# Block means of V as products with a constant matrix, in a three-stage attention and feed-forward kernel

## The chip, the cores and the metric

The kernel runs on one core of a Trainium2 chip. The metric is the device time of one execution in microseconds. TensorE (PE in the profile) does the matrix products, VectorE (DVE), ScalarE (ACT) and GpSimd (POOL) the element-wise work, and SyncE (SP) issues nearly all loads and stores.

## The reference, cut to what matters

```python
B, H, S, D = 2, 8, 768, 64;  block, window = 32, 16
k_sum = k.reshape(B, H, 24, 32, D).max(axis=3)      # block maxima
v_sum = v.reshape(B, H, 24, 32, D).mean(axis=3)     # block means
scores_l = q @ k.T / 8      # kept where |i - j| < 16, else -1e9
scores_s = q @ k_sum.T / 8 + log(32)
a = softmax(concat(scores_l, scores_s))
x = a @ concat(v, v_sum)                            # 1536 x 512 over both batches
h = x @ w_in;  x = (h - tanh(h)) @ w_out            # 512 -> 2048 -> 512
xn = rms_norm(x) * rms_g
out = (silu(xn @ w_gate) * (xn @ w_val)) @ w_out2   # 512 -> 1536 -> 512
```

The change touches only the block means of V in the first batch, the order of the block maxima of K in the second, and the order of the first loads.

## The kernel before, in words

**Attention.** The 1536 rows are twelve tiles of 128 queries, six for each batch. A *unit* is one tile and one parity of the heads (four heads): unit 2i is tile i with parity 0, unit 2i+1 the same tile with parity 1. `scores(u)` multiplies the tile's queries (a load `q` of 512 KB for each tile) with a window of 96 keys and the 24 block maxima (`kw`), four heads of 120 columns each, in true 32-bit (L347; each product is two instructions on PE). VectorE adds the mask and takes the row's extreme (L350), ScalarE takes the exponential (L352), VectorE finishes the sums (L353, L354), GpSimd scales (L355). `trans(u)` turns the result on PE (L362), ScalarE copies it out (L367), and `pv(i)` multiplies both parities with the tile's window of V (`v`, L379). `pv` writes x as a rounded half (ScalarE, L382) and a remainder (VectorE, L383).

**Block maxima of K.** `ksum_a(b, par, hf)` loads half the tiles of one parity (`kw`, 576 KB) and takes the maxima on VectorE (L264, two L266, L267). `ksum_b` spreads them over the partitions by two products with a selection matrix (L273), and VectorE and GpSimd write them into `kw`. No unit of a parity can start before both halves of its maxima.

**Block means of V.** `vsum_a(b, c)` loads a quarter of V (`vt`, 384 KB, features on the partitions) and adds up 32 neighbours. For the first batch quarters 0, 2 and 3 are one VectorE reduction each (L295), and quarter 1 is a tree of additions on GpSimd (L291, L293). `vsum_b` turns the four quarters on PE (L301), and ScalarE (L305) and VectorE (L307) scale by 1/32 and write the 24 rows into the tile's `v`. `pv(0)` needs both.

**Feed-forward.** Weights come as 64-bit words and are decoded into two rounded parts: ScalarE L163, VectorE L164, L165 and L166, the rounding on VectorE (L173, the first four pieces) or ScalarE (L171), the remainder on GpSimd (L174). Loads of weights go through three buffers `raw`. `up_step` (L396 to L398) is a product of 384 columns for a group of three tiles, so the first needs `pv` of tiles 0, 1 and 2 and the first decoded weight; `down_step` (L402 to L404) has 512 columns. Both are in the rounded format, one instruction for each product.

**Order.** Each task has a due time in `plan`; tasks are emitted in the order of their due times, each behind the tasks that it requires. A scheduler with a timeline model then fixes each engine's order at build time, and each engine runs its list in order. Loads that wait for nothing go out in the order of emission. The first four units are due in the order 0, 2, 1, 3 (`ORD`), at 6, 9.5, 13 and 15.5; unit 4 is due at 18.

Of the kernel before, what the change touches and what calls it, by code (L numbers as in the profile page):

```python
# [2 lines left out]

# [50 lines left out]
TP1 = 1.0  # L54
TC = 0.6
TK01 = 1
TV = 4
TK1 = -8
TV1 = -8
TD0 = 11  # L60
# [6 lines left out]
PSV = 0  # L67
PTV = 0
KBUF = 4
PVS = (1, 1)  # L70
PB = 4
PTB = 3
SHIFT = {}
ALT = ()
OSA = 6
SSH = 8
TSEL = 0.3
TQ = (0.2, 3)
TVL = (6, 16)
ORD = [0, 2, 1, 3]  # L80
TKB = (4, 6)
VE = ((0, 1, 0, 0), (1, 1, 1, 1))
DTV = 0.25
TVS = 10
TCKW = {"schedule_with_timeline_sim": True}


# [1 line left out]
def attn_moe_kernel(ctx: ExitStack, tc: tile.TileContext, ins, out, dbg=None):  # L89
    nc = tc.nc  # L90
    V, A, G, T = nc.vector, nc.scalar, nc.gpsimd, nc.tensor

    cst = ctx.enter_context(tc.tile_pool(name="cst", bufs=1))
    wp = ctx.enter_context(tc.tile_pool(name="wp", bufs=SLOTS_A))
# [9 lines left out]
    ps_t = att_ctx.enter_context(tc.tile_pool(name="ps_t", bufs=PST, space=PSUM))  # L104
    ap1 = att_ctx.enter_context(tc.tile_pool(name="ap1", bufs=1))
# [3 lines left out]
    kp_ = att_ctx.enter_context(tc.tile_pool(name="kp", bufs=KBUF))  # L109
    sa = att_ctx.enter_context(tc.tile_pool(name="sa", bufs=4))  # L110
    rawp = att_ctx.enter_context(tc.tile_pool(name="rawp", bufs=RB))
    state = {}

    def f(ap):
        return ap.bitcast(F32)

    sel = cst.tile([128, 256], F32, name="sel")
    ident = sel[:, 64:192]
    rg = cst.tile([128, KD], F32, name="rg")
    mask = ap1.tile([128, 3, WID], F32, name="mask")  # L120


    def consts():
        nc.sync.dma_start(out=mask, in_=ins["mask"])
        nc.sync.dma_start(out=rg, in_=ins["rms_g"])


    jobs = []
# [120 lines left out]
    def ksum_a(b, par, hf):  # L249
        if not kwin:  # L250
            for h2 in range(2):
                for p2 in range(2):
                    kwin[0, p2, h2] = kp_.tile([128, KT, 4 * WID], F32, name="kw")
        if b:
            kwin[b, par, hf] = kp_.tile([128, KT, 4 * WID], F32, name="kw")
        kw = kwin[b, par, hf]
        m1 = ap2.tile([128, KT, 2, 4], F32, name="m1")
        m2 = ap2.tile([128, KT, 2, 4], F32, name="m2")
        if not hf:
            kmax[b, par] = ap2.tile([128, 4, TPB, 2], F32, name="mx")  # L260
        ts = slice(hf * KT, hf * KT + KT)
        nc.sync.dma_start(out=kw[:, :, 0:4 * LOC], in_=ins["kw"][b, par, :, ts])
        w = kw[:, :, 0:4 * LOC].rearrange("p t (j k c) -> p t j k c", j=4, k=4)
        V.tensor_reduce(m1.rearrange("p t j k -> p t (j k)"), kw[:, :, 96:288].rearrange("p t (x c) -> p t x c", c=24), AX.X, ALU.max)  # L264
        for j in range(2):
            V.tensor_reduce(m2[:, :, j], w[:, :, 3 * j, :, 16:24], AX.X, ALU.max)  # L266
        V.tensor_tensor(kmax[b, par][:, :, ts].rearrange("p k t j -> p t j k"), m1, m2, ALU.max)  # L267

    def ksum_b(b, par):
        mx = kmax.pop((b, par)).rearrange("p k t j -> p (k t j)")  # L270
# [5 lines left out]
        G.tensor_copy(sm[:, 1:], sm[:, 0:1].to_broadcast([128, KT - 1, 96]))  # L276
        G.tensor_copy(sm2, sm[:, 0:1].to_broadcast([128, KT, 96]))

    def vsum_a(b, c, pool, name):
# [3 lines left out]
        raw = pool.tile([128, 1024], U32, name=name) if name == "raw" else pool.tile([128, 2, 512], F32R, name=name).rearrange("p a n -> p (a n)")  # L283
        rr = f(raw)[:, 0:S]
        nc.sync.dma_start(out=rr, in_=ins["vt"][b, c])
        r = rr.rearrange("p (n j) -> p n j", j=BLK)
        o = vt_[b][:, c, LOC:]
        if VE[b][c]:
            n = BLK // 2
            while n > 1:  # L290
                G.tensor_tensor(r[:, :, 0:n], r[:, :, 0:n], r[:, :, n:2 * n], ALU.add)  # L291
                n //= 2
            G.tensor_tensor(o, r[:, :, 0], r[:, :, 1], ALU.add)  # L293
        else:
            V.tensor_reduce(o, r, AX.X, ALU.add)  # L295

    def vsum_b(b):
        vt = vt_.pop(b)
        ps = ps_t.tile([128, 512], F32, name="t")
        for c in range(4):  # L300
            T.transpose(ps[0:WID, c * 128:(c + 1) * 128], vt[:, c], ident)  # L301
        if b == 0:
            v_of[0] = 0
            vsum[b] = v_b[0][LOC:WID, 0]
            A.activation(v_b[0][LOC:WID, 0], ps[LOC:WID], AF.Copy, scale=1.0 / BLK)  # L305
            if PVS[b]:
                V.tensor_scalar(v_b[0][LOC:WID, 1], ps[LOC:WID], 1.0 / BLK, None, ALU.mult)  # L307
            else:
                A.activation(v_b[0][LOC:WID, 1], ps[LOC:WID], AF.Copy, scale=1.0 / BLK)
            return  # L310
        vsum[b] = ap1.tile([128, DM], F32, name="vsum")[LOC:WID]
        if PVS[b]:
            V.tensor_scalar(vsum[b], ps[LOC:WID], 1.0 / BLK, None, ALU.mult)
        else:
            A.activation(vsum[b], ps[LOC:WID], AF.Copy, scale=1.0 / BLK)
# [18 lines left out]
    def scores(u):  # L334
        b, t, par = unit(u)
        q = q_b[(u // 2) % QB]
        kw = kwin[b, par, t // KT][:, t % KT].rearrange("p (j k c) -> p j k c", j=5, k=4)
        mk = mask[:, 1 if 0 < t < TPB - 1 else (0 if t == 0 else 2)]
        P = Pp.tile([128, 4, WID], F32, name="P")
        nb = sp.tile([128, 4], F32, name="nb")  # L340
        sm = sp.tile([128, 4], F32, name="sm")
        nh = 2 if (u < S2) != (f"sh{u}" in ALT) else 4
        for k0 in range(0, 4, nh):
            ps = ps_h.tile([128, 512], F32, name="h") if u < SSH else ps_t.tile([128, 512], F32, name="t")
            for i in range(nh):
                k = k0 + i
                T.matmul(ps[:, i * WID:(i + 1) * WID], q[:, 4 * par + k], kw[:, :, k], start=True, stop=True)  # L347
            for i in range(nh):
                k = k0 + i
                V.tensor_tensor_reduce(P[:, k], ps[:, i * WID:(i + 1) * WID], mk, -0.125, 3e38, ALU.add, ALU.min, nb[:, k:k + 1])  # L350
# [37 lines left out]
    for j, nch in enumerate(NCH):  # L388
# [4 lines left out]
    acc, part, gs, last = {}, {}, {}, {}  # L393
# [200 lines left out]
    def task(key, at, fn, *req):  # L594
        plan[key] = (at + SHIFT.get(key, 0), len(plan), fn, req)
# [48 lines left out]
    at = TM0  # L644
# [61 lines left out]
    for i in range(n0, len(steps) + LAG):  # L706
# [18 lines left out]
        j, g, m, first, end = steps[i - LAG]  # L725
# [5 lines left out]
        if j == len(NCH) - 1 and end:  # L731
            t = free["t"]
# [33 lines left out]
        down2(*prev, j)  # L766


_INS = ["q", "kw", "vt", "vw", "mask", "sel", "rms_g", "w_in", "w_out", "w_gate", "w_val", "w_out2"]


def layouts(q, k, v, moe_w_in, moe_w_out, moe2_w_gate, moe2_w_val, moe2_w_out, moe2_rms_g):
# [15 lines left out]
    vt = v.transpose(0, 2, 1, 3).reshape(B, S, DM)  # L788
# [45 lines left out]
```

## Time and profile before

| what | us |
|---|---|
| median of three runs | 655.16 (654.47 to 655.91) |
| the profiled execution | 655.48 |
| its span, first to last instruction | 653.7 |
| PE busy | 625.3 (96% of the span) |
| VectorE busy | 455.1 (70%) |
| ScalarE busy | 325.6 (50%) |
| GpSimd busy | 232.4 (36%) |

Busy time is an average over stages with different limits: which engine or transfer ends the waits has to be read for each stretch by itself. A busy PE may also be one that runs at half its clock.

### The profile page before, as it was taken

How to read it: one execution, taken by the hardware profiler on the slowest of the kernel's cores; microseconds unless marked ns; L12 is line 12 of the kernel's file. 1: busy time of each engine (PE TensorE's matmuls, PEld its weight loads, DVE VectorE, ACT ScalarE, POOL GpSimd, SP SyncE). 2: the span in 40 equal slices, each digit the busy share in tenths (PEclk: the TensorE clock that was granted, in tenths of full speed). 3: DMA queues.
4: the chain of work that ended last, by engine and by line, in shares of the span. 5: the costliest groups of instructions: out<-in, count | busy, mean ns of one | idle time of the engine just before them, and what ended most of it. 6: DMA issues, size and time to landing. Idle time of an engine off the chain costs nothing.

```text
span 653.7 us, 9841 instructions
## 1 busy us (share of the span) xinstructions
PE 625.3 (96%) x3576; PEld 570.3 (87%) x3576; DVE 455.1 (70%) x979; ACT 325.6 (50%) x783; POOL 232.4 (36%) x237
## 2 busy tenths in 40 slices
PE   3878999999999999999999899999999999999997
PEld 3768898889999999999998887999999999999995
DVE  5899755458777667766458488676778768778644
ACT  2865576545543444444456765454544544454420
POOL 1467721113231223441000026545626645555300
PEclk9878999999999999999999899999999999999999
DMA  9986321123222223111000001021111211111013
GB/s 331 348 259 238 110 99 50 46 77 130 99 107 85 100 94 129 66 65 64 1 2 0 2 33 65 33 98 64 66 65 64 97 66 64 66 66 64 2 65 128
DMA packets 19641, 58.92 MB, mean 90 GB/s; under 512 B 2168, under 2 KB 5496, under 8 KB 19592
## 3 DMA queue, kind: packets, MB, share of 16 engines
q1 hardware_dynamic: 19592, 58.29, 25.9%
q8 instruction: 28, 0.46, 0.3%
q14 instruction: 21, 0.17, 0.1%
HBM read 54.84 MB, written 3.15 MB: 89 GB/s over the span
## 4 chain that ended last, share of the span: by engine, by line
PE 74%; issue 12%; DVE 9%; ACT 2%; DMA 1%; POOL 1%; SPq 0%; DVEq 0%; POOLq 0%
PE h L398 7%; PE h L396 7%; PE h L397 7%; PE acc L403 5%; PE acc L402 5%; PE acc L404 5%; PE t L402 5%; PE t L403 5%; PE t L404 5%; PE acc L396 4%; PE acc L397 4%; PE acc L398 4%; PE accx L397 2%; PE accx L396 2%; PE accx L398 2%
## 5 line engine op out<-in xcount | busy, mean ns | idle before, releaser
L174 POOL TENSOR_TENSOR w<-dt,w 128x512 fp32r<-128x512 f32 (+1 forms) x59 | 75.8, 1284 | 147.0 <-ACT w L171 120.6
L398 PE MATMUL h<-x,w 128*128 128x384 f32 x248 | 84.3, 341 | 2.2 <-DVE x L383 2.2
L396 PE MATMUL h<-x,w 128*128 128x384 f32 x248 | 85.0, 343 | 0.9 <-ACT x L382 0.9
L397 PE MATMUL h<-x,w 128*128 128x384 f32 x248 | 84.3, 340 | 0.0
L414 ACT ACTIVATE s<-h 128x384 f32<-128x384 f32 x64 | 31.2, 487 | 75.9 <-PE h L398 75.6
L415 DVE TENSOR_TENSOR s<-h,s 128x384 f32<-128x384 f32 x64 | 35.5, 554 | 40.8 <-ACT s L414 40.2
L396 PE MATMUL acc<-x,w 128*128 128x384 f32 x168 | 57.6, 343 | 2.7 <-ACT s L530 1.9
L165 DVE SCALAR_TENSOR_TENSOR dt<-da,dt 128x512 uint32<-128x512 uint32 x68 | 55.9, 823 | 5.2 <-ACT da L163 1.4
L418 DVE TENSOR_TENSOR g<-s,g 128x384 fp32r<-128x384 f32 x64 | 44.5, 696 | 21.5 <-ACT g L417 21.4
L438 DVE TENSOR_TENSOR part<-t,part 128x512 f32<-128x512 f32 x60 | 40.5, 686 | 26.3 <-PE t L404 26.1
L397 PE MATMUL acc<-x,w 128*128 128x384 f32 x168 | 57.3, 341 | 0.0
L166 DVE SCALAR_TENSOR_TENSOR dt<-raw,dt 128x512 uint32<-128x512 uint32 x68 | 56.1, 826 | 1.3
L403 PE MATMUL acc<-w,g 128*128 128x512 f32 x144 | 57.0, 396 | 0.0
L403 PE MATMUL t<-w,g 128*128 128x512 f32 x144 | 56.8, 395 | 0.0
L404 PE MATMUL t<-w,g 128*128 128x512 f32 x144 | 56.7, 393 | 0.0
L404 PE MATMUL acc<-w,g 128*128 128x512 f32 x144 | 56.4, 396 | 0.0
L398 PE MATMUL acc<-x,w 128*128 128x384 f32 x168 | 56.3, 340 | 0.0
L402 PE MATMUL t<-w,g 128*128 128x512 f32 x144 | 55.2, 397 | 1.1 <-DVE part L436 0.8
L402 PE MATMUL acc<-w,g 128*128 128x512 f32 x144 | 54.5, 395 | 0.0
L526 DVE TENSOR_TENSOR g<-s,g 128x384 fp32r<-128x384 f32 x48 | 33.4, 708 | 25.9 <-ACT g L525 25.9
L352 ACT ACTIVATE P<-P,nb 128x120 f32<-128x120 f32 x96 | 36.8, 384 | 28.2 <-DVE nb L350 27.7
L396 PEld LDWEIGHTS h<-x,w 128*128 128x128 f32 x248 | 47.1, 190 | 3.6 <-ACT x L382 1.3
(130 smaller groups left out, 1556.7 us busy)
## 6 DMA issues: line engine op xcount, KB each, us to landing
raw<-w_out SPq DMA_DIRECT2D x28, 512.0 KB, 3.2
raw<-w_in SPq DMA_DIRECT2D x16, 512.0 KB, 3.8
q<-q SPq DMA_DIRECT2D x12, 512.0 KB, 7.6
raw<-w_gate SPq DMA_DIRECT2D x12, 512.0 KB, 3.1
raw<-w_val SPq DMA_DIRECT2D x12, 512.0 KB, 3.4
kw<-kw SPq DMA_DIRECT2D x8, 576.0 KB, 6.7
v<-vw SPq DMA_DIRECT2D x12, 384.0 KB, 5.1
out_dram<-part SPq DMA_DIRECT2D x12, 256.0 KB, 2.0
```

Of the source, the lines that this page charges most:

```text
L165: V.scalar_tensor_tensor(t, a.bitcast(U32), 3, t, ALU.logical_shift_left, ALU.bitwise_or)
L166: V.scalar_tensor_tensor(t, r[:, :, 1], 0x80000000, t, ALU.bitwise_and, ALU.bitwise_or)
L174: G.tensor_tensor(lo, d, f(hi), ALU.subtract)
L352: A.activation(P[:, k], P[:, k], AF.Exp, scale=-1.0, bias=nb[:, k:k + 1], accum_out=sm[:, k:k + 1])
L396: T.matmul(o, wh, xh, start=start, stop=False, **kw)
L397: T.matmul(o, wl, xh, start=False, stop=False, **kw)
L398: last["PE"] = T.matmul(o, wh, xl, start=False, stop=stop, **kw)
L402: T.matmul(o, g[:, 0, js], w[:, 0], start=first, stop=False)
L403: T.matmul(o, g[:, 1, js], w[:, 0], start=False, stop=False)
L404: last["PE"] = T.matmul(o, g[:, 0, js], w[:, 1], start=False, stop=end)
L418: last["DVE"] = V.tensor_tensor(gg[:, 1], t, f(gg[:, 0]), ALU.subtract)
L438: V.tensor_tensor(part[t], a, part[t], ALU.add)
```

## The change

The block means of the first batch are no longer reduced on VectorE and GpSimd. V is loaded in its natural layout, keys on the partitions, in three pieces `vn` of 512 KB, and each of the six tiles of 128 keys is multiplied by a slice of a constant matrix `mean` (128 x 130, holding 1/32 at the right places). The six products of 512 columns, in true 32-bit, add up in one accumulator; ScalarE and VectorE copy it out as before, without the scaling. `tc.issue_after(ins)` puts the instructions of its block behind `ins` in the order of that instruction's engine; it adds no semaphore. The six products are put behind the last score product emitted so far, which with the due time 15.6 is that of the fourth unit; the maxima of the second batch are put behind the last L350 emitted so far.

The loads change order. Before: `kw` (parity 0, first half), `q` of tile 0, `kw` (second half), `sel`, `mask`, `rg`, two `kw` of parity 1, `q` of tile 1, four `vt`, `vw` of tile 0, `q` of tile 2, weights. After: `kw` first half on SyncE and second half on ScalarE's queue, `sel`, `q` of tile 0, `mask`, two `kw` of parity 1, `mean`, three `vn`, `vw` of tile 0, `q` of tile 1, `q` of tile 2, weights; `rg` at 20.

```diff
-TV = 4
+TV = 1.5
-TSEL = 0.3
-TQ = (0.2, 3)
-TVL = (6, 16)
+TSEL = 0.15
+TQ = (0.4, 3)
+TVL = (2.6, 16)
-TVS = 10
+TVS = 15.6
...
 def ksum_a(b, par, hf):
-        nc.sync.dma_start(out=kw[:, :, 0:4 * LOC], in_=ins["kw"][b, par, :, ts])
+        (nc.scalar if not (b or par) and hf else nc.sync).dma_start(out=kw[:, :, 0:4 * LOC], in_=ins["kw"][b, par, :, ts])
-        V.tensor_reduce(m1...); V.tensor_reduce(m2...) x2; V.tensor_tensor(kmax...)
+        with tc.issue_after(last["SC"].ins) if b else nullcontext():
+            (the same four)
...
 def vsum_a(b, c):
+        if b == 0:
+            vn[c] = wp.tile([128, 2, 512], F32R, name="w")
+            nc.sync.dma_start(out=f(vn[c]), in_=ins["vn"][c])
+            return
...
 def vsum_b(b):
+        if b == 0:
+            with tc.issue_after(last["QK"].ins):
+                for t in range(TPB):
+                    T.matmul(ps[0:WID], mean[:, 2 * (TPB - 1 - t):2 * (TPB - 1 - t) + WID], f(vn[t // 2])[:, t % 2], start=(t == 0), stop=(t == TPB - 1))
+            A.activation(v_b[0][LOC:WID, 0], ps[LOC:WID], AF.Copy)
+            V.tensor_copy(v_b[0][LOC:WID, 1], ps[LOC:WID])
+            return
...
-        task(f"ka0{par}{hf}", at + hf / 4, ...)
+        task(f"ka0{par}{hf}", at + hf / 10, ...)
-    for c in range(4):
-        task(f"va0{c}", TV + c * DTV, lambda c=c: vsum_a(0, c, wp, "w"))
-    task("vs0", TV * 0 + TVS, lambda: vsum_b(0), "sel", *[f"va0{c}" for c in range(4)])
+    for c in range(3):
+        task(f"va0{c}", TV + c * DTV, lambda c=c: vsum_a(0, c))
+    task("mean", TV - 0.1, lambda: nc.sync.dma_start(out=mean, in_=ins["mean"]))
+    task("rg", 20, lambda: nc.sync.dma_start(out=rg, in_=ins["rms_g"]))
+    task("vs0", TVS, lambda: vsum_b(0), "mean", *[f"va0{c}" for c in range(3)])
```

## Rows read from the trace of the kernel before

**Rows 1.** Windows; columns PE, PEld, DVE, ACT, POOL, granted clock, DMA share, GB/s.
```profile
10.00:20.00 10.00, 8.73 (x38) 7.96 (x38) 8.36 (x41) 4.43 (x22) 5.01 (x9) 1.00 1.04 367
20.00:30.00 10.00, 7.20 (x50) 6.85 (x50) 8.69 (x37) 9.24 (x35) 4.07 (x6) 0.94 1.04 358
30.00:40.00 10.00, 7.16 (x67) 6.18 (x68) 8.98 (x41) 5.60 (x21) 5.80 (x5) 0.67 1.05 317
40.00:50.00 10.00, 8.83 (x120) 7.65 (x116) 9.76 (x27) 7.46 (x24) 5.81 (x4) 0.87 0.73 234
60.00:70.00 10.00, 9.74 (x81) 8.70 (x80) 9.70 (x31) 4.86 (x15) 8.37 (x11) 1.00 0.49 192
...
120.00:300.00 180.00, 180.00 (x957) 162.24 (x956) 124.55 (x204) 80.74 (x159) 51.42 (x43) 1.00 0.25 89
```

**Rows 2.** Timeline of PE: start, time, what, count, and the wait before it.
```profile
13.25 2.03 PE L347 MATMUL h<-kw,q 128*128 128x120 f32 x8 [0.52 <-DMA q<-q]
...
19.35 3.24 PE L347 MATMUL h<-kw,q 128*128 128x120 f32 x16
...
22.86 0.49 PE L301 MATMUL t<-sel,vt 128*120 128x128 f32 x3
...
30.52 1.93 PE L379 MATMUL acc<-pt,v 120*64 120x64 f32 x30
...
51.66 0.44 PE L398 MATMUL h<-x,w 128*128 128x384 f32 x1 [2.24 <-DVE x L383]
```

**Rows 3.** Timeline of VectorE, the operations that the sum speaks of.
```profile
7.86 0.75 DVE L264 TENSOR_REDUCE m<-kw 128x24 f32<-128x576 f32 x1 [1.83 <-DMA kw<-kw]
...
21.31 0.28 DVE L350 CUSTOM_DVE_ANT_0 P<-h,mask 128x120 f32<-128x120 f32 x1
...
22.19 0.92 DVE L164 TENSOR_SCALAR dt<-raw 128x512 uint32<-128x512 uint32 x1
...
33.51 0.74 DVE L264 TENSOR_REDUCE m<-kw 128x24 f32<-128x576 f32 x1
...
50.95 0.65 DVE L383 TENSOR_TENSOR x<-acc,x 128x512 fp32r<-128x512 f32 x1
```

**Rows 4.** Groups by line and shape in the first 62 us: busy and mean ns.
```profile
L166 DVE SCALAR_TENSOR_TENSOR dt<-raw,dt 128x512 uint32<-128x512 uint32 x7 | 6.8, 966 | 0.0
L164 DVE TENSOR_SCALAR dt<-raw 128x512 uint32<-128x512 uint32 x7 | 6.1, 869 | 0.0
...
L264 DVE TENSOR_REDUCE m<-kw 128x24 f32<-128x576 f32 x7 | 5.2, 741 | 4.9 <-DMA kw<-kw 4.9
L165 DVE SCALAR_TENSOR_TENSOR dt<-da,dt 128x512 uint32<-128x512 uint32 x7 | 5.0, 718 | 0.2
...
L266 DVE TENSOR_REDUCE m<-kw 128x12 f32<-128x96 f32 x14 | 2.9, 240 | 0.0
L295 DVE TENSOR_REDUCE vt<-w 128x24 f32<-128x768 f32 x3 | 2.8, 942 | 0.0
...
L173 DVE CAST w<-dt 128x512 fp32r<-128x512 f32 x4 | 1.7, 420 | 0.0
...
L267 DVE TENSOR_TENSOR mx<-m,m 128x24 f32<-128x24 f32 x7 | 1.4, 195 | 0.1
```

**Rows 5.** Chain of waits, one unit's eight score instructions at the full clock: start, time.
```profile
87.61 0.89 PE t L347 x8
```

**Rows 6.** Timeline of PE, first and last of nine products of 512 columns, rounded format.
```profile
302.91 0.40 PE L402 MATMUL acc<-x,g 128*128 128x512 f32 x1
...
304.78 0.40 PE L404 MATMUL acc<-x,g 128*128 128x512 f32 x1
```

**Rows 7.** Short windows of the core, columns as in Rows 1.
```profile
36.00:38.00 2.00, 1.48 (x7) 1.48 (x8) 2.00 (x8) 2.00 (x9) 1.28 (x2) 0.50 1.07 346
38.00:40.00 2.00, 2.00 (x21) 1.79 (x21) 1.01 (x8) 0.40 (x2) 1.41 (x2) 0.50 1.04 223
40.00:42.00 2.00, 2.00 (x28) 1.88 (x25) 2.00 (x9) 1.78 (x8) 0.94 (x1) 0.50 0.44 131
```

More of the change, by code (lines that the diff above doesn't have):

```diff
@@ L1 @@
 import heapq
-from contextlib import ExitStack
+from contextlib import ExitStack, nullcontext
 import concourse.bass as bass
@@ L69 @@
 KBUF = 4
-PVS = (1, 1)
 PB = 4
@@ L76 @@
 SSH = 8
-TSEL = 0.3
-TQ = (0.2, 3)
-TVL = (6, 16)
+TSEL = 0.15
+TQ = (0.4, 3)
+TVL = (2.6, 16)
 ORD = [0, 2, 1, 3]
 TKB = (4, 6)
-VE = ((0, 1, 0, 0), (1, 1, 1, 1))
 DTV = 0.25
-TVS = 10
+TVS = 15.6
 TCKW = {"schedule_with_timeline_sim": True}
@@ L111, in attn_moe_kernel @@
     rawp = att_ctx.enter_context(tc.tile_pool(name="rawp", bufs=RB))
-    state = {}
+    state, last = {}, {}
     def f(ap):
@@ L120, in attn_moe_kernel @@
     mask = ap1.tile([128, 3, WID], F32, name="mask")
+    mean = ap1.tile([128, WID + 2 * (TPB - 1)], F32, name="mean")
     def consts():
         nc.sync.dma_start(out=mask, in_=ins["mask"])
-        nc.sync.dma_start(out=rg, in_=ins["rms_g"])
     jobs = []
@@ L261, in ksum_a @@
         ts = slice(hf * KT, hf * KT + KT)
-        nc.sync.dma_start(out=kw[:, :, 0:4 * LOC], in_=ins["kw"][b, par, :, ts])
+        (nc.scalar if not (b or par) and hf else nc.sync).dma_start(out=kw[:, :, 0:4 * LOC], in_=ins["kw"][b, par, :, ts])
         w = kw[:, :, 0:4 * LOC].rearrange("p t (j k c) -> p t j k c", j=4, k=4)
[L264 to L267, printed above, removed]
+        with tc.issue_after(last["SC"].ins) if b else nullcontext():
+            V.tensor_reduce(m1.rearrange("p t j k -> p t (j k)"), kw[:, :, 96:288].rearrange("p t (x c) -> p t x c", c=24), AX.X, ALU.max)
+            for j in range(2):
+                V.tensor_reduce(m2[:, :, j], w[:, :, 3 * j, :, 16:24], AX.X, ALU.max)
+            V.tensor_tensor(kmax[b, par][:, :, ts].rearrange("p k t j -> p t j k"), m1, m2, ALU.max)
     def ksum_b(b, par):
@@ L277, in ksum_b, with vsum_a @@
         G.tensor_copy(sm2, sm[:, 0:1].to_broadcast([128, KT, 96]))
-    def vsum_a(b, c, pool, name):
+    vn = {}
+    def vsum_a(b, c):
+        if b == 0:
+            vn[c] = wp.tile([128, 2, 512], F32R, name="w")
+            nc.sync.dma_start(out=f(vn[c]), in_=ins["vn"][c])
+            return
         if c == 0:
@@ L282, in vsum_a @@
             V.memset(vt_[b][:, :, 0:LOC], 0.0)
-        raw = pool.tile([128, 1024], U32, name=name) if name == "raw" else pool.tile([128, 2, 512], F32R, name=name).rearrange("p a n -> p (a n)")
-        rr = f(raw)[:, 0:S]
-        nc.sync.dma_start(out=rr, in_=ins["vt"][b, c])
+        rr = f(rawp.tile([128, 1024], U32, name="raw"))[:, 0:S]
+        nc.sync.dma_start(out=rr, in_=ins["vt"][c])
         r = rr.rearrange("p (n j) -> p n j", j=BLK)
[L287 to L295, printed above, removed]
@@ L297, in vsum_b @@
-    def vsum_b(b):
+        n = BLK // 2
+        while n > 1:
+            G.tensor_tensor(r[:, :, 0:n], r[:, :, 0:n], r[:, :, n:2 * n], ALU.add)
+            n //= 2
+        G.tensor_tensor(vt_[b][:, c, LOC:], r[:, :, 0], r[:, :, 1], ALU.add)
+    def vsum_b(b):
+        ps = ps_t.tile([128, 512], F32, name="t")
+        if b == 0:
+            with tc.issue_after(last["QK"].ins):
+                for t in range(TPB):
+                    T.matmul(ps[0:WID], mean[:, 2 * (TPB - 1 - t):2 * (TPB - 1 - t) + WID], f(vn[t // 2])[:, t % 2], start=(t == 0), stop=(t == TPB - 1))
+            v_of[0] = 0
+            vsum[b] = v_b[0][LOC:WID, 0]
+            A.activation(v_b[0][LOC:WID, 0], ps[LOC:WID], AF.Copy)
+            V.tensor_copy(v_b[0][LOC:WID, 1], ps[LOC:WID])
+            return
@@ L298, in vsum_b @@
         vt = vt_.pop(b)
-        ps = ps_t.tile([128, 512], F32, name="t")
         for c in range(4):
             T.transpose(ps[0:WID, c * 128:(c + 1) * 128], vt[:, c], ident)
[L302 to L310, printed above, removed]
@@ L311, in vsum_b @@
         vsum[b] = ap1.tile([128, DM], F32, name="vsum")[LOC:WID]
[L312 to L315, printed above, removed]
+        V.tensor_scalar(vsum[b], ps[LOC:WID], 1.0 / BLK, None, ALU.mult)
     def qload(i):
@@ L346, in scores @@
                 k = k0 + i
-                T.matmul(ps[:, i * WID:(i + 1) * WID], q[:, 4 * par + k], kw[:, :, k], start=True, stop=True)
+                last["QK"] = T.matmul(ps[:, i * WID:(i + 1) * WID], q[:, 4 * par + k], kw[:, :, k], start=True, stop=True)
             for i in range(nh):
                 k = k0 + i
-                V.tensor_tensor_reduce(P[:, k], ps[:, i * WID:(i + 1) * WID], mk, -0.125, 3e38, ALU.add, ALU.min, nb[:, k:k + 1])
+                last["SC"] = V.tensor_tensor_reduce(P[:, k], ps[:, i * WID:(i + 1) * WID], mk, -0.125, 3e38, ALU.add, ALU.min, nb[:, k:k + 1])
         for k in range(4):
@@ L392, in attn_moe_kernel @@
         m0 += nch
-    acc, part, gs, last = {}, {}, {}, {}
+    acc, part, gs = {}, {}, {}
     def triple(o, wh, wl, xh, xl, start, stop, **kw):
@@ L612, in attn_moe_kernel @@
         for hf in range(2):
-            task(f"ka0{par}{hf}", at + hf / 4, lambda par=par, hf=hf: ksum_a(0, par, hf))
+            task(f"ka0{par}{hf}", at + hf / 10, lambda par=par, hf=hf: ksum_a(0, par, hf))
         task(f"kb0{par}", TKB[par], lambda par=par: ksum_b(0, par), f"ka0{par}0", f"ka0{par}1", "sel")
-    for c in range(4):
-        task(f"va0{c}", TV + c * DTV, lambda c=c: vsum_a(0, c, wp, "w"))
-    task("vs0", TV * 0 + TVS, lambda: vsum_b(0), "sel", *[f"va0{c}" for c in range(4)])
+    for c in range(3):
[3 more added lines that the diff above has]
+    task("vs0", TVS, lambda: vsum_b(0), "mean", *[f"va0{c}" for c in range(3)])
     at = t_sc(2 * TPB)
@@ L624, in attn_moe_kernel @@
     for c in range(4):
-        task(f"va1{c}", at + TV1 + 3 * c, lambda c=c: vsum_a(1, c, rawp, "raw"))
+        task(f"va1{c}", at + TV1 + 3 * c, lambda c=c: vsum_a(1, c))
     task("vs1", at + TV1 + 14, lambda: vsum_b(1), *[f"va1{c}" for c in range(4)])
@@ L766, in attn_moe_kernel @@
         down2(*prev, j)
-_INS = ["q", "kw", "vt", "vw", "mask", "sel", "rms_g", "w_in", "w_out", "w_gate", "w_val", "w_out2"]
+_INS = ["q", "kw", "vn", "vt", "vw", "mean", "mask", "sel", "rms_g", "w_in", "w_out", "w_gate", "w_val", "w_out2"]
 def layouts(q, k, v, moe_w_in, moe_w_out, moe2_w_gate, moe2_w_val, moe2_w_out, moe2_rms_g):
@@ L805, in layouts @@
         mask[:, i, LOC:] = 8.0 * np.log(BLK)
+    mean = np.zeros((128, WID + 2 * (TPB - 1)), np.float32)
+    mean[np.arange(128), LOC + 2 * (TPB - 1) + 2 * TPB * (np.arange(128) // 64) + np.arange(128) // BLK % 2] = 1.0 / BLK
     return {
@@ L808, in layouts @@
         "kw": np.ascontiguousarray(kw).reshape(B, 2, 128, TPB, 4 * LOC),
-        "vt": np.ascontiguousarray(vs), "vw": np.ascontiguousarray(vw),
+        "vt": np.ascontiguousarray(vs[1]), "vn": np.ascontiguousarray(vt[0].reshape(TPB // 2, 2, 128, DM).transpose(0, 2, 1, 3)),
+        "mean": mean, "vw": np.ascontiguousarray(vw),
         "mask": mask,
```

## The prediction

> **What bounds the kernel now.** I read first the windows of the core [rows 1]. From 120 to 300 us PE is busy for the whole stretch at a granted clock of 1.00: that part is TensorE's, and the change leaves it alone. The change lives in the first 60 us. There PE is not the bound: from 10 to 50 us it stands idle for 1.27 + 2.80 + 2.84 + 1.17 = 8.1 us, and part of its busy time is at half clock (0.67 in the window from 30 to 40). VectorE is: 8.4 to 9.8 of every 10 us from 10 to 50, and 9.7 still from 60 to 70. The transfers are the second bound up to 40 us, with a share of 1.04 and about 360 GB/s.
>
> The timelines come second, for what waits. On PE the second unit begins at 13.25 after a wait for the load of `q` of tile 1; the dense feed-forward stream begins at 51.66, after 2.24 us of waiting for VectorE's L383, the remainder of x of tile 2 [rows 2]. That L383 runs at 50.95 [rows 3], although its unit's scores were long done: it stands behind whatever VectorE has in its list. So the number to follow is how much work VectorE has ahead of that L383. After 51.66 PE is nearly full, and a microsecond gained there is a microsecond at the end, unless PE gets more to do.
>
> **The change, part by part.**
>
> *V sums off VectorE.* Three reductions of 0.942 us [rows 4] go: 2.83 us. What replaces L307's scaling is a copy of the same 24 x 512 elements, counted as equal. GpSimd's tree for one quarter goes too; GpSimd is busy 5 to 6 of 10 us there [rows 1] and I count nothing for it. The 2.83 us can end up between nothing and all of it, and the next part decides.
>
> *Load order.* Behind the two `kw` of parity 1 now stand `mean` (65 KB), three `vn` (1536 KB) and one `vw` (384 KB) before `q` of tile 1: 1985 KB, or 2.03 MB, which at 367 GB/s [rows 1] is 5.5 us. `q` of tile 1 was there at 13.25 [rows 2], so now at 18.8. Units 2 and 3 need it. Unit 1 needs only tile 0 and moves ahead, if the scheduler sees this. At the early rate of 2.03 us for a unit [rows 2] unit 2 is through PE at 20.8 and unit 3 at 22.8; VectorE ends unit 3's four L350 (0.28 and less each) about 0.9 us later, at 23.7. Before, unit 3's L350 began at 21.31 [rows 3], and with the same 0.9 us it ended at 22.2. So four units are done 1.5 us later than before, though VectorE lost 2.83 us of work: it idles until 18.8 with nothing to take. The first weight is no later (the bytes ahead of it are the same but for 65 KB), and its first VectorE step came at 22.19 [rows 3]; in the new order VectorE can do some 1 us of that decoding in between. So most of the 2.83 us is spent on waiting. Bounds for what is left are 0 and 2.83; I take 0.5, near the lower one, because the idle time stands in the very stretch where the reductions stood. The first half-load of `kw` moved to ScalarE's queue may bring unit 0 up to 1.3 us earlier (VectorE waited 1.83 us for it, until 7.86 [rows 3]), but units 2 and 3 still meet `q` at 18.8, so it counts nothing. `rg` is wanted only in the third stage: nothing.
>
> *Six products instead of four transposes.* True 32-bit products are two instructions each, so twelve of 512 columns. No such row exists. Lower bound: nine 512-column products in the rounded format follow each other from 302.91 to 304.78, 0.234 us each [rows 6]; twelve are 2.8 us. Upper bound: eight 120-column instructions of a unit's scores take 0.89 us at the full clock [rows 5], 0.111 each; scaled by 512/120 it is 0.475, and twelve are 5.7 us, or 11.4 at half clock. I take the upper row, which is of the same format. The transposes gone are worth some 0.5 us (three in 0.49 [rows 2]). The products stand on PE behind unit 3 and, by due time (15.6 against 18), before unit 4. They begin at 22.8 and end between 28.5 and 34.2. Queued behind them are the scores of units 4 and 5, the transposes L362, and `pv(0)`, which also waits for their result; `pv(0)` ran at 30.52 before [rows 2], about when the new result is there if the clock rises midway (some 8 us, to 31). What hides them is PE's own idle time of 8.1 us and VectorE's backlog: in three `raw` buffers there are three weights to decode at 0.869 + 0.718 + 0.966 + 0.420 = 2.97 us each [rows 4], 8.9 us of work that needs nothing of PE, from about 22 to 31. So I count the products as 0; without that cover they cost what is beyond 31, up to 3.2 us.
>
> On the price the Trainium skill says the same against this change: the page FP8 and Floating Point Precision, section TensorE Precision Notes, counts four passes of the array for a true 32-bit product. As an estimate from that page six products would be 6 x 4 x 512 columns at 2.4 GHz, 5.1 us, and 10.2 at 1.2 GHz; the rows give 5.7 and 11.4. By either the sum keeps its 0 for them at the full clock, and by the 2.8 us of the lower row the slower rival below would hardly exist; so the page is a reason to leave that rival its chance.
>
> *Maxima of the second batch tied.* One half is 0.741 + 2 x 0.240 + 0.195 = 1.42 us on VectorE [rows 4]. Two halves ran from 33.51 on [rows 3], before the scores of units 7 and 8, and so ahead of the L383 at 50.95. They are now behind the L350 of units 8 and 9, and those units' scores come later, being behind the six products. Between none and both of the halves fall behind that L383: 0 to 2.83 us. One of the two is due later than `pv(2)` and tied to the later unit, so I take one, 1.4. Units of the second batch need them only from unit 12 on. The tie is an order and adds no semaphore.
>
> *Sum.* 0.5 + 1.4 + 0 = 1.9 us less than the profiled execution's 655.48, so 653.6. That execution lies 0.3 above the median of 655.16, which gives 653.3 for the median.
>
> **Rivals.**
>
> *No change.* VectorE is still at 9.7 of 10 from 60 to 70 [rows 1]. If x is ready earlier but the maxima then take their 2.8 us from the feed-forward's own VectorE steps, the start is only shuffled, and the 0.5 us is all: 654.7, within 0.2% (1.3 us), which is about what a measurement of this kernel can tell from no change. For it speaks that the work on VectorE after 23 us is the same list; against it that PE was idle at the very wait for L383.
>
> *Slower: the products run at half clock.* Then PE is held from 22.8 to 34.2. VectorE's 8.9 us of weights are done at 31, and it idles 3.2 us; units 4 and 5, which decide `pv(2)`, are late by that. It decides from the point at which the products end later than 31. Price: 3.2 less the 1.4 of the tie, with the 0.5 lost as well, +1.8: 657.0. For it speaks that the same scores took 2.03 us at 13.25 against 0.89 later [rows 2, 5], which means that PE ran at 1.2 GHz up to then (the clock column says 1.00 there; the instructions' own times contradict it). Against it: eight us of unbroken products are more than PE ever had in that stretch.
>
> *Faster still: the products keep PE's clock up.* In the windows from 36 to 42 the granted clock is 0.50, with 1.48 + 2.00 + 2.00 us busy [rows 7], after PE had been idle in part before. At full clock that work would take 2.7 us less. It holds the products `pv(1)` and `pv(2)`, so x of tile 2 would come up to 2.7 us earlier, if VectorE is free for its L383; since VectorE is full I count at most the 2.24 us that PE waited there [rows 2]: 653.3 - 2.2 = 651.1. The Trainium skill has the rule behind this in TensorE: Matmul & The Clock Gate, Part 1: the throttled clock is the default, and activity of the array releases it. The trace agrees in so far as the clock is 0.50 there after slack windows and 1.00 in the dense part.
>
> **How the numbers follow.** Forecast (1.3 to 3 us gained, 652.2 to 653.9) 0.40; no change 0.28; slower 0.22; faster still 0.10. So faster by over 0.2%: 0.50; within 0.2%: 0.28; slower: 0.22. The range: below, all of 2.83 + 2.83 us gained gives 655.16 - 5.7 = 649.5; above, 3.2 us uncovered with nothing gained gives 658.4. With a tenth left out on the upper side I take 649.6 to 657.7.
>
> **What would show it.** Right: PE has twelve 512-column instructions from about 23 us, ending before 31; `q` of tile 1 is waited for until about 18.8; VectorE does weights in that time; the first L264 of the second batch stands after unit 8's L350; PE's dense stream begins before 50.5 with a shorter wait for L383. Wrong: the products end past 31 and VectorE idles before unit 4; or `q` of tile 1 holds unit 1 too because PE's list still has unit 2 before it, which would cost up to a unit's time more; or the stream begins earlier and PE then waits for VectorE's L415 and L418 between 52 and 70, so that nothing is gained.

## The result, and the profile after

The changed kernel takes 661.11 us (median of four, 660.45 to 661.59); four runs of the kernel before, on the same chip, took 654.47 to 655.91. The ratio is 1.0087, with an interval of 1.0074 to 1.0099: slower by 5.7 us (the two medians differ by 6.1). The forecast was 653.3, its range 649.6 to 657.7: a gain was forecast, and the kernel lost. The profiled span went from 653.7 to 659.4 us, at the same mean clock of 0.99.

The windows come first, in the columns of [rows 1]:

```profile
10.00:20.00 10.00, 5.45 (x21) 4.60 (x22) 3.70 (x19) 2.31 (x9) 2.42 (x5) 1.00 1.04 374
20.00:30.00 10.00, 9.86 (x40) 6.37 (x39) 8.53 (x30) 6.22 (x21) 3.41 (x3) 1.00 0.78 268
30.00:40.00 10.00, 4.47 (x32) 3.74 (x31) 9.90 (x22) 4.05 (x13) 5.53 (x4) 0.70 0.78 267
40.00:50.00 10.00, 6.26 (x76) 5.43 (x74) 9.36 (x45) 8.63 (x36) 6.73 (x7) 0.84 0.93 266
60.00:70.00 10.00, 10.00 (x89) 9.23 (x88) 9.09 (x23) 5.50 (x15) 8.44 (x12) 1.00 0.81 266
```

Between 10 and 20 us VectorE lost 2.83 us of reductions. Had it done the rest of its work, it would have been busy for 8.36 - 2.83 = 5.5 us; it was busy for 3.70. PE lost 3.3 us there, filled the next window to 9.86 with the products, and then was busy for only 4.47 of 10 us from 30 to 40, against 7.16 before. PE's timeline (start, time, what, count, the wait before it) says why:

```profile
13.97 1.09 PE L272 MATMUL t<-mx,sel 128*128 128x48 f32 x4 [1.90 <-DVE mx L266]
15.18 1.11 PE L359 MATMUL t<-sel,P 128*120 128x128 f32 x4
18.81 4.26 PE L344 MATMUL h<-kw,q 128*128 128x120 f32 x16 [2.52 <-DMA q<-q]
22.86 5.71 PE L302 MATMUL t<-w,mean 128*120 128x512 f32 x12
28.42 1.49 PE L344 MATMUL h<-kw,q 128*128 128x120 f32 x12
...
35.71 0.45 PE L376 MATMUL acc<-pt,v 120*64 120x64 f32 x2 [4.14 <-DMA v<-v]
37.54 2.06 PE L344 MATMUL h<-kw,q 128*128 128x120 f32 x8 [1.39 <-DVE nb L347]
...
56.65 0.42 PE L395 MATMUL h<-x,w 128*128 128x384 f32 x1
```

The load of `q` of tile 1 holds PE until 18.81, and the products run from 22.86 for 5.71 us. Both stand where the prediction put them. What it did not have is the size of what waits around them. The 16 score instructions at 18.81 are unit 2 and then unit 1, although unit 1 does not need that load. The dense stream, whose first instruction that needs the remainder of x of tile 2 was L398 at 51.66 [rows 2] and is L395 now, starts at 56.65: 5.0 us late, most of the 5.7. VectorE's timeline shows the same gaps from its side:

```profile
15.10 0.26 DVE L274 COPY kw<-t 128x96 f32<-128x96 f32 x1 [1.11 <-PE t L272]
20.91 0.28 DVE L347 CUSTOM_DVE_ANT_0 P<-h,mask 128x120 f32<-128x120 f32 x1 [5.56 <-PE h L344]
...
21.73 0.42 DVE L162 TENSOR_SCALAR dt<-raw 128x512 uint32<-128x512 uint32 x1
...
23.32 0.69 DVE L163 SCALAR_TENSOR_TENSOR dt<-da,dt 128x512 uint32<-128x512 uint32 x1
...
35.86 0.70 DVE L306 COPY v<-t 24x512 f32<-24x512 f32 x1
36.59 0.28 DVE L347 CUSTOM_DVE_ANT_0 P<-h,mask 128x120 f32<-128x120 f32 x1
...
53.86 0.74 DVE L263 TENSOR_REDUCE m<-kw 128x24 f32<-128x576 f32 x1
55.55 0.68 DVE L380 TENSOR_TENSOR x<-acc,x 128x512 fp32r<-128x512 f32 x1
```

The copy at 15.10 is about the last thing that unit 1 needed (in e5 below, where it need not stand in line, it starts on PE at 15.94); VectorE then idles for 5.56 us, until unit 2's scores. Unit 3's scores start on PE at 28.42, but VectorE takes them at 36.59, behind the weights that its list has first and behind the copy of the block means (L306), which had its products at 28.6. The remainder of x is at 55.55, where it was at 50.95 [rows 3].

### The profile page after: what moved, and what is told of

Read it like the earlier page. It is cut to its first block, busy times and chain, and to the rows that moved or that the text cites. A ratio compares the mean times of both kernels' runs of the same rounds, so it can differ in the third digit from the quotient of the medians.

```text
span 659.4 us, 9843 instructions
## 1 busy us (share of the span) xinstructions
PE 627.1 (95%) x3584; PEld 568.1 (86%) x3584; DVE 454.4 (69%) x975; ACT 325.0 (49%) x783; POOL 230.5 (35%) x232
## 4 chain that ended last, share of the span: by engine, by line
PE 76%; issue 12%; DVE 7%; DMA 3%; ACT 1%; POOL 1%; SPq 0%; DVEq 0%; POOLq 0%
PE h L393 7%; PE h L394 7%; PE h L395 7%; PE acc L400 5%; PE acc L401 5%; PE acc L399 5%; PE t L399 5%; PE t L400 5%; PE t L401 5%; PE acc L393 4%; PE acc L395 4%; PE acc L394 4%; PE accx L393 2%; PE accx L394 2%; PE accx L395 2%
## 5 line engine op out<-in xcount | busy, mean ns | idle before, releaser
L395 PE MATMUL h<-x,w 128*128 128x384 f32 x248 | 83.6, 338 | 0.0
L163 DVE SCALAR_TENSOR_TENSOR dt<-da,dt 128x512 uint32<-128x512 uint32 x68 | 57.3, 844 | 5.2 <-ACT da L161 1.6
L415 DVE TENSOR_TENSOR g<-s,g 128x384 fp32r<-128x384 f32 x64 | 44.0, 687 | 21.8 <-ACT g L414 21.7
L395 PE MATMUL acc<-x,w 128*128 128x384 f32 x168 | 56.3, 340 | 0.0
L414 ACT ACTIVATE g<-s 128x384 fp32r<-128x384 f32 x64 | 33.5, 524 | 32.4 <-DVE s L412 31.5
```

Source lines behind the costliest of these rows:

```text
L163: V.scalar_tensor_tensor(t, a.bitcast(U32), 3, t, ALU.logical_shift_left, ALU.bitwise_or)
L395: last["PE"] = T.matmul(o, wh, xl, start=False, stop=stop, **kw)
L415: last["DVE"] = V.tensor_tensor(gg[:, 1], t, f(gg[:, 0]), ALU.subtract)
```

## The theories

**A (load order and lists).** The late `q` of tile 1 is what costs: unit 1 waits behind unit 2 on PE, VectorE idles, and unit 3's scores then meet a VectorE list that has weights first. **B (products).** The 5.7 us of products on PE, ahead of unit 3, cost more than the idle time covers. **C (place).** They cost because they stand behind three units, not behind four. **D (tie).** The tied maxima are in the way. In the expectations, which were written before each run, theory L is the late load of A, theory M the part of A that VectorE's list has, and theory P is B (in e3 it is C). They call a run by its number: the second run is e2.

The table gives the median, the ratio to runs of the kernel before that were timed with it, its interval, and the start of PE's first instruction that needs the third remainder, the remainder of x of tile 2, in the profiled execution (e13's was 3 us above its median and is left out). Differences between kernels are taken from the ratios. Each edit lets the scheduler fix all the lists anew, so what a run gains belongs to its edit with all that the edit moves.

| kernel | median us | ratio [interval] | start |
|---|---|---|---|
| before | 655.0 to 655.9 | 1 | 51.66 |
| changed | 661.11 | 1.0087 [1.0074, 1.0099] | 56.65 |
| e1 before, load order alone | 657.41 | 1.0028 [1.0018, 1.0038] | 54.05 |
| e2 changed, `q` early | 654.76 | 0.9990 [0.9982, 0.9999] | 49.80 |
| e3 changed, behind four units | 663.81 | 1.0129 [1.0116, 1.0142] | 59.35 |
| e4 changed, no tie of maxima | 664.92 | 1.0151 [1.0131, 1.0172] | 61.01 |
| e5 changed, unit 1 first | 657.97 | 1.0037 [1.0023, 1.0052] | 53.34 |
| e6 changed, one product | 659.07 | 1.0050 [1.0036, 1.0064] | 55.05 |
| e7 before, tie of maxima | 654.39 | 0.9977 [0.9968, 0.9986] | 51.19 |
| e8 `q` early, behind four | 654.65 | 0.9994 [0.9982, 1.0006] | 48.04 |
| e9 changed, weights tied | 659.78 | 1.0061 [1.0049, 1.0073] | 55.47 |
| e10 `q` early, weights tied | 652.24 | 0.9945 [0.9933, 0.9957] | 46.13 |
| e11 `q` early, one product | 652.35 | 0.9951 [0.9938, 0.9964] | 45.79 |
| e12 before, tie, `kw` on ScalarE's queue | 653.68 | 0.9963 [0.9950, 0.9977] | 48.12 |
| e13 unit 1 first, weights tied | 656.75 | 1.0033 [1.0020, 1.0046] | - |
| e14 e12, weights tied | 653.08 | 0.9971 [0.9957, 0.9984] | 49.97 |

One per cent is 6.6 us. A later start is mostly a later end, but not one for one: e10 starts 5.5 us before the kernel before, and its span is 3.2 us shorter (650.5).

## Experiments: the late load

**e1: the new load order in the kernel before.** The sums of V stay as they were.

```diff
-TV = 4
+TV = 1.5
-TSEL = 0.3
-TQ = (0.2, 3)
-TVL = (6, 16)
+TSEL = 0.15
+TQ = (0.4, 3)
+TVL = (2.6, 16)
```

(and the second half of each first `kw` closer behind the first half, that of parity 0 on ScalarE's queue, and `rg` later.)

> The kernel before with the new order of the first loads alone (V still summed on VectorE and GpSimd, four loads of V in the place of the three; no products, no ties). Theory L (the late load of q of tile 1 starves VectorE and PE until 18.8 us, and that is the loss): 658 to 661 us, first score product of unit 2 at about 18.8 us. Theory P (the six products, 5.6 us more of PE work in a kernel that PE bounds, standing ahead of unit 3): within 1.5 us of 655.

It costs 1.8 us (0.28%), more than nothing and less than the whole loss, between the two ranges expected. PE waits for the same `q`, but before that VectorE has the three reductions to do, so it is busy for 6.38 us between 10 and 20 us where the changed kernel has 3.70. PE and the window in e1:

```profile
18.59 2.92 PE L346 MATMUL h<-kw,q 128*128 128x120 f32 x12 [1.38 <-DMA q<-q]
```

```profile
10.00:20.00 10.00, 5.78 (x23) 4.88 (x24) 6.38 (x22) 2.32 (x9) 4.70 (x10) 1.00 1.04 372
```

**e2: the changed kernel with `q` of tile 1 ahead of the V loads.**

```diff
-TQ = (0.4, 3)
+TQ = (0.4, 1.3)
```

> The changed kernel with one number different: q of tile 1 is due at 1.3 instead of 3, so it is loaded ahead of mean and the three pieces of V. Theory L: most of the loss of 6 us goes, 655 to 657 us; VectorE's wait of 5.6 us before unit 2 is gone. Theory P: 659 to 661 us, since the products and their place ahead of unit 3 stay.

One number gives back 6.4 us (1.0087 to 0.9990), the whole loss. The code of the products and the ties is the same; the lists, fixed anew, have the products at 18.24 and not at 22.86. The window, PE and VectorE's first step of a weight in e2:

```profile
10.00:20.00 10.00, 8.91 (x37) 7.67 (x38) 6.11 (x39) 5.53 (x25) 3.37 (x6) 1.00 1.04 371
```

```profile
13.12 2.03 PE L344 MATMUL h<-kw,q 128*128 128x120 f32 x8 [1.09 <-DMA q<-q]
...
18.24 5.35 PE L302 MATMUL t<-w,mean 128*120 128x512 f32 x12
...
49.80 0.44 PE L395 MATMUL h<-x,w 128*128 128x384 f32 x1 [0.43 <-DVE x L380]
```

```profile
21.38 0.43 DVE L162 TENSOR_SCALAR dt<-raw 128x512 uint32<-128x512 uint32 x1 [1.30 <-DMA raw<-w_in]
```

VectorE is back at 6.11 us, a little over the 5.5 that were worked out above. So the late load is worth 6.4 us here and 1.8 in e1. (e1 also has half of `kw` on the second queue, whose gain of up to 0.9 us is not shown, see e12; the load alone may cost that much more there.) That it costs less in e1 because there VectorE can fill the wait is borne out by the account behind e14, though the two kernels also differ in the products and the tie.

**e5: unit 1 ahead of unit 2.**

```diff
-ORD = [0, 2, 1, 3]
+ORD = [0, 1, 2, 3]
```

> The changed kernel with the first four units due in the order 0, 1, 2, 3 instead of 0, 2, 1, 3: q of tile 1 is as late as before (18.8 us), but unit 1, which does not need it, no longer stands behind unit 2 on PE. If the waiting of unit 1 in line is what the late load costs: VectorE's idle time before 20.9 us shrinks from 5.6 to about 4 us, and 657 to 659.5 us. If the lateness of units 2 and 3 themselves is what costs: 660 to 662 us.

With `q` as late as ever (PE waits until 19.05 in e5) it gives back 3.3 us, over half of the loss. Unit 1 runs in the wait, and VectorE's idle time before unit 2's scores, 5.56 us in one piece, becomes 4.5 in four:

```profile
15.94 1.90 PE L344 MATMUL h<-kw,q 128*128 128x120 f32 x8
19.05 2.03 PE L344 MATMUL h<-kw,q 128*128 128x120 f32 x8 [1.21 <-DMA q<-q]
20.87 5.90 PE L302 MATMUL t<-w,mean 128*120 128x512 f32 x12
```

**e9 and e13: the weights' VectorE steps tied behind the last scores emitted**, in the changed kernel and together with e5's order.

```diff
-        V.tensor_scalar(t, r[:, :, 0], 29, None, ALU.logical_shift_right)
...
+        with tc.issue_after(last["SC"].ins) if "SC" in last else nullcontext():
+            V.tensor_scalar(t, r[:, :, 0], 29, None, ALU.logical_shift_right)
...
```

> The changed kernel with VectorE's three steps of decoding each weight put behind the last L350 emitted so far, so that in VectorE's list the third and later weights no longer stand ahead of units 3 and 4 (whose scores are on PE by 29 us and were taken at 36.6 us). Theory M (VectorE's fixed list, made for products that end later than they do, is half of the loss): 656.5 to 659 us and unit 3 taken before 32 us. If the list only mirrors that VectorE is full: 660 to 662 us.

> The changed kernel, q of tile 1 still late, with both edits of lists: units due in the order 0, 1, 2, 3 and the weights tied behind the scores on VectorE. If the late load costs only through the two fixed lists: their gains add up (3.1 and 1.6 us), 655.5 to 657 us or less, and what is left above the tenth run (652.2) is under 4 us. If the lateness of units 2 and 3 costs beside the lists: 657.5 to 659 us.

In e9 VectorE takes unit 3's scores at 31.77 and not at 36.59, and the copy of the means in the same stretch at 31.05:

```profile
31.05 0.70 DVE L307 COPY v<-t 24x512 f32<-24x512 f32 x1 [1.58 <-ACT v L306]
31.77 0.28 DVE L348 CUSTOM_DVE_ANT_0 P<-h,mask 128x120 f32<-128x120 f32 x1
```

These 4.8 us there are worth 1.7 us at the end (1.0087 to 1.0061), less than theory M asked for. With both orders mended (e13, 1.0033) the gain is 3.5 us. The intervals can tell that neither from e5's gain alone nor from the sum 3.3 + 1.7. What is left above e10's time is 4.5 us, by the ratios 5.8, where under 4 was expected if the lists alone cost.

**e10: `q` early and the weights tied.** The edits of e2 and e9.

> The second run's kernel (q of tile 1 loaded early) with the same tie of the weights. Theory M: little left to gain, 653.5 to 655 us. If the list only mirrors that VectorE is full: 654.5 to 656 us.

652.24 us, 0.55% faster than the kernel before, better than either range, and the fastest measured together with e11, which leaves work out. The third remainder is at 44.87, where the changed kernel has it at 55.55. Against e9 the early load is worth 7.6 us (1.0061 to 0.9945), against e13 5.8. So the late load costs most of its price even where both lists suit it; the lists are not the whole of A.

```profile
44.87 0.66 DVE L381 TENSOR_TENSOR x<-acc,x 128x512 fp32r<-128x512 f32 x1
```

**e14: is that the tie of the weights alone?** The kernel before with the tie of the maxima, the `kw` load on ScalarE's queue (both in e12) and the weights tied.

> The twelfth run's kernel (the kernel before, maxima tied, half of kw on ScalarE's queue; V summed on VectorE and GpSimd) with the weights tied as well; against the tenth run (652.2) it differs in how the block means are made. If the products are worth their place when all else is right: 652.5 to 654 us. If VectorE's sums are the better way: 650.5 to 652 us.

0.9971 against 0.9963 of e12: no difference beyond the intervals. The tie of the weights gives 1.7 us (e9) and 2.9 us (e10 against e2) in the changed kernel and none that can be seen in this one.

**VectorE's account up to the third remainder.** These are the windows from 10 us to the start of the third remainder, for the changed kernel, e1, e2, e5, e9 and e10, in this order (VectorE's busy time is the third column of busy times):

```profile
10.00:55.55 45.55, 31.59 (x227) 25.39 (x228) 36.53 (x130) 25.71 (x92) 23.63 (x25) 0.89 0.84 280
10.00:51.88 41.88, 28.77 (x228) 25.45 (x228) 36.83 (x143) 26.14 (x99) 21.00 (x23) 0.90 0.90 306
10.00:49.07 39.07, 31.41 (x264) 25.76 (x266) 33.35 (x139) 26.66 (x97) 22.19 (x22) 0.96 1.04 331
10.00:52.12 42.12, 32.83 (x228) 26.32 (x229) 33.35 (x131) 26.36 (x93) 23.87 (x23) 0.84 0.91 298
10.00:54.52 44.52, 34.60 (x240) 27.53 (x242) 31.22 (x134) 25.78 (x96) 19.81 (x22) 0.88 0.87 284
10.00:44.87 34.87, 29.40 (x226) 23.98 (x227) 29.01 (x126) 23.84 (x90) 17.72 (x17) 0.90 1.04 346
```

The length less the busy time is what VectorE idled: 9.0, 5.1, 5.7, 8.8, 13.3 and 5.9 us. e1 has as much work ahead of the third remainder as the changed kernel, idles 4.0 us less and reaches it 3.7 us earlier: there the wait was filled. The load made early (changed kernel to e2) brings it 6.5 us forward, 3.3 of them idle time and 3.2 work that no longer stands ahead; with the weights tied (e9 to e10) 9.7 us, 7.4 of them idle time. So the late load costs VectorE waiting in each pair. e5 is another matter: it brings the third remainder 3.4 us forward, but only 0.25 of that is idle time. The same 25 steps of weights stand ahead of it, and they take 18.0 us and not 21.8; the last section shows what the long ones have in common.

## Experiments: products and place

**e6 and e11: one product of the six**, in the changed kernel and in e2. Five sixths of the keys are left out of the first batch's means; loads, copies and order stay.

```diff
-                for t in range(TPB):
+                for t in (0,):
```

> The changed kernel with one of the six products left out five times (only the first tile's product stays, so the block means miss five sixths of their keys); loads and all else as in the changed kernel. It takes 4.7 us of work off PE between 23 and 28 us. Theory P: 656 to 657.5 us. Theory L: the products are hidden behind VectorE, 659 to 661 us.

> The second run's kernel (q of tile 1 loaded early) with one product instead of six (five sixths of the block means' keys left out): the price of the products where nothing else is late. If PE's idle time hides them: 654 to 655.3 us. If they cost as they did in the changed kernel (2 to 2.5 us): 652 to 653 us.

```profile
22.72 1.02 PE L302 MATMUL t<-w,mean 128*120 128x512 f32 x2
```

PE has 4.7 us less to do (1.02 for 5.71), and the kernel gains 2.4 us with `q` late (1.0087 to 1.0050) and 2.6 us with `q` early (0.9990 to 0.9951). e6's median lies at the foot of theory L's range and not in theory P's, but the gain is beyond the intervals. So B holds for some 2.5 us in either order: about half of the products is covered, half is not.

**e3 and e8: the products behind four units**, with `q` late and with `q` early.

```diff
-    task("vs0", TVS, lambda: vsum_b(0), "mean", *[f"va0{c}" for c in range(3)])
+    task("vs0", TVS, lambda: vsum_b(0), "sc3", "mean", *[f"va0{c}" for c in range(3)])
```

> The changed kernel with the products made to require the scores of unit 3, so that they stand behind four units; in the changed kernel they stand behind three, since the fill of the tile of V is due at 14 and pulls them forward. Theory P in its form that the place is what costs: 656 to 659 us, VectorE takes unit 3 at about 24 us instead of 36.6. Theory L: 660 to 661 us, nearly no change.

> The changed kernel with q of tile 1 loaded ahead of mean and V and with the products behind four units (the edits of the second and third run together). If the place behind unit 3 was bad only because unit 3 was late: 653 to 655 us, below the second run's 654.8. If the place behind unit 3 costs by itself: 656 to 658 us.

With `q` late it is 2.8 us slower still; with `q` early it makes no difference (0.9994 against 0.9990, intervals almost the same). Theory C falls. VectorE takes unit 3's scores at 25.73 in e3, 10.9 us before it does in the changed kernel, and the time is longer still: unit 3's place behind the weights, the third part of theory A, is not by itself the price. In e3 the products start 1.6 us later than in the changed kernel, and PE's transposes later wait 3.79 us for the copy L306, which VectorE has behind weights, at 35.73 as against 35.86 in the changed kernel:

```profile
18.74 5.97 PE L344 MATMUL h<-kw,q 128*128 128x120 f32 x24 [2.54 <-DMA q<-q]
24.50 5.39 PE L302 MATMUL t<-w,mean 128*120 128x512 f32 x12
...
36.58 1.08 PE L359 MATMUL t<-sel,P 128*120 128x128 f32 x4 [3.79 <-DVE v L306]
```

```profile
25.73 0.27 DVE L347 CUSTOM_DVE_ANT_0 P<-h,mask 128x120 f32<-128x120 f32 x1
...
35.73 0.70 DVE L306 COPY v<-t 24x512 f32<-24x512 f32 x1
```

## Experiments: the tie of the maxima

**e4 and e7: the tie taken out of the changed kernel, and put into the kernel before.**

```diff
-        with tc.issue_after(last["SC"].ins) if b else nullcontext():
+        with nullcontext():
```

> The changed kernel without the tie of the second batch's maxima. If the tie matters (a third theory): 2 us or more away from 661. Theories L and P both: 660 to 662 us.

> The kernel before with the tie of the second batch's maxima alone. By the changed kernel without it (3.8 us slower) the tie is worth 1 to 4 us: 651 to 654 us. If its worth comes only from the late units of the changed kernel: 654.5 to 656 us.

The tie gains in both: 1.5 us in the kernel before, 4.2 us in the changed one (1.0151 to 1.0087). D falls; without the tie the loss would be 9.9 us. VectorE in e4 has reductions of the maxima at 43.57 and 48.65, ahead of the third remainder, which is at 60.07:

```profile
43.57 0.74 DVE L263 TENSOR_REDUCE m<-kw 128x24 f32<-128x576 f32 x1
...
48.65 0.72 DVE L263 TENSOR_REDUCE m<-kw 128x24 f32<-128x576 f32 x1
...
60.07 0.68 DVE L380 TENSOR_TENSOR x<-acc,x 128x512 fp32r<-128x512 f32 x1
```

**e12: the kernel before with the tie and half of the first `kw` on ScalarE's queue.**

> The kernel before with the tie of the maxima and with the second half of the first parity's kw issued on ScalarE's queue; V is still summed on VectorE and GpSimd and q of tile 1 stays early. It adds to the seventh run the 0.6 us earlier start of unit 0. If that start counts: 653 to 654 us. If not: 654 to 655 us.

0.9963 against e7's 0.9977; the intervals overlap, so the 0.9 us of the second queue is not shown.

## Why the prediction was wrong, point by point

**The step that failed is the load order**, which the prediction let eat 2.3 of the 2.83 us saved on VectorE and then closed. It had the time of the load right (18.8 worked out, 18.81 measured) and the idle VectorE right. It went wrong in one sentence: "Unit 1 needs only tile 0 and moves ahead, if the scheduler sees this". It did not. Unit 1 stayed behind unit 2 on PE's list, which was the second case of the list of what would make the prediction wrong, priced there at up to a unit's 2 us, with no term in the sum, no chance and no part in the range; e5 makes it 3.3 us. So of the four units that were to be through VectorE at 23.7 three were, half a microsecond late, and the fourth, unit 3, was begun at 36.59. What was said of the weights came about: some 1 us of decoding in between was forecast, and VectorE did 0.42 + 0.69 us of it by 24 us. It could not have begun much before 21.7, since in e2 VectorE waits for the first weight's load until 21.38. The measured price of the late load is 6.4 us (e2) against 2.3. Half of it goes with the order of the units (e5), 1.7 us with the place of the weights (e9), and against e10 the load still costs 5.8 us with both mended (e13). How those 5.8 us are made up was not separated; in e9 and e10, which differ in the load alone, three quarters of the difference at the third remainder is VectorE waiting.

**V sums.** The term (0.5 of 2.83 us) could only be worth something where VectorE has other work in the stretch. With `q` early and only one product to pay for, e11 is 0.12% below e12, whose intervals overlap; 0.5 us is neither shown nor excluded. With `q` late, VectorE's saving turned into idle time, as e1 and the changed kernel show side by side: 6.38 and 3.70 us busy from 10 to 20 us.

**Products.** Start 22.8 and 5.7 us at the full clock were forecast; 22.86 and 5.71 were measured. The start was forecast for four units ahead of the products, and came with three, because unit 1 ran where unit 3 was counted. The 5.7 is in part luck: it scaled 0.111 us for 120 columns [rows 5] to 0.475 for 512, but the twelve instructions follow each other 0.43 us apart (in e10 their starts run from 17.8 to 22.5), about 5.15 in all. The rest of the 5.71 is the first instruction, which takes 0.99 us, and the end of the last. The estimate of 5.1 us by the four passes of the Trainium skill (FP8 and Floating Point Precision, TensorE Precision Notes) agrees with the 5.15. The rows are of e10 and of the changed kernel:

```profile
L303 PE MATMUL t<-w,mean x12: 592/592/595, 17.8 to 22.5; 128*120 128x512 f32 x12
L302 PE MATMUL t<-w,mean x12: 592/592/994, 22.9 to 28.0; 128*120 128x512 f32 x12
```

(the durations are the shortest, the median and the longest, in ns.)

The step "I count the products as 0" failed by 2.4 to 2.6 us (e6, e11). They end at 28.6, before the 31 that the cover was to last, and VectorE's weights lasted longer than worked out (about 13.5 us of steps between 21.73 and 35.83, against 8.9), so there was cover enough by that reckoning and it did not cover. VectorE's copy of the products' result, L306, stands behind those weights in its list, at 35.86. Which of the works behind the products (unit 3, the transposes, that copy, `pv(0)`) hands the 2.5 us on was not tried. That they stand "behind unit 3", and behind the fourth unit in the section on the change, was misread: `vf0`, due at 14, requires `vs0` and so pulls it ahead of its own 15.6 and of unit 3's 15.5. This did no harm (e3, e8).

**Maxima.** 1.4 us was forecast with the right sign: 1.5 in the kernel before, 4.2 in the changed one. As forecast, one of the two halves falls behind the third remainder (L263 at 53.86 and then at 57.11, the remainder at 55.55). Why the tie is worth more in the changed kernel was not tried.

**The sum.** With `q` early the terms come near: e2 is 0.7 us faster than the kernel before, where -1.9 was forecast for all parts, and the products' 2.6 us more than account for the difference.

**The rivals.** *Slower* had the right side and the wrong mechanism: the products were at full clock, but for the first instruction, and ended before its point of 31, and 657.0 was 4 us short. *Faster still* did not happen: the granted clock from 30 to 40 us is 0.70 after and 0.67 before [rows 1], after PE had stood idle for 4.14 us, and the next eight scores take 2.06 us, as at 1.2 GHz. That agrees with the Trainium skill (TensorE: Matmul & The Clock Gate, Part 1), by which the throttled clock is the default.

**Open.** Whether products in place of reductions are worth having by themselves depends on the lists: with `q` early they are 0.27% worse than e12, with the weights tied too 0.26% better than e14. These pairs also differ in the order of the V loads. A rival was left untried: VectorE's copy of the means (L306, in e9 L307), moved ahead of the weights by itself. With `q` late it stands at 35.86 in the changed kernel, 31.05 in e9, 28.93 in e6 and 27.89 in e5, and the times fall in that order; but each of these edits moves other work too.

## What to carry to other kernels

A load that is made later must be priced by all that stands behind its first consumer on each engine's fixed list, not by that consumer alone: here an independent unit stood behind it. Work taken off an engine is worth nothing in a stretch in which that engine then waits: the same late load cost 1.8 us in a kernel with work to fill the wait and 6.4 us in one from which that work had been moved away. Another engine's backlog may be no cover for new work whose result has to pass through the same backlog. A due time holds only if nothing due earlier requires the task; follow the requirements before placing it.

## What the runs showed of the hardware that was not expected

A product of 512 columns in true 32-bit is two instructions, 0.43 us apart at the full clock (e10), 1.8 times the 0.234 of the rounded format [rows 6]. The clock column says 1.00 in the changed kernel's windows up to 30 us, yet sixteen scores take 4.26 us at 18.81 and twelve take 1.49 at 28.42; the instructions' own times tell the level.

One product (two instructions) waited 4.14 us on PE, until 35.71, by the profile for a copy `v<-v` (48 KB) that brings the means from ScalarE's copy into another tile's `v`. ScalarE had written it by 30.0; SyncE issued the copy at 31.93, behind two loads of weights. Short work late on one list can hold an engine as long as a large load:

```profile
29.16 2.72 SPq L155 DMA_DIRECT2D raw<-w_out  x2
31.93 1.66 SPq L329 DMA_DIRECT2D v<-v  x2
```

Steps of a weight on VectorE with the same shape take very different times. Of the 25 ahead of the third remainder in the changed kernel, 17 take 0.41 to 0.69 us and eight take 1.20 to 1.75. Seven of these eight begin while an instruction runs on GpSimd and end 0.3 to 0.6 us after it, as here in the changed kernel; that the one holds up the other was not tried.

```profile
27.09 1.45 POOL L172 TENSOR_TENSOR w<-dt,w 128x512 fp32r<-128x512 f32 x1 [0.36 <-DVE sm L350]
27.34 1.75 DVE L164 SCALAR_TENSOR_TENSOR dt<-raw,dt 128x512 uint32<-128x512 uint32 x1
```
